# A new hand-fixed order of instructions and transfers in a two-branch state-space kernel

## The chip, the cores and the metric

One core of one Trainium2 chip. The metric is the device time of one execution in microseconds (us), taken over several runs; lower is better. Beside it stands one profiled execution, from which all rows of the trace come.

## The reference

Two independent branches, A and B, on 2048 time steps and 640 channels, are computed and put side by side in one output of 2048 x 1280 in bf16.

Branch A is a diagonal complex state-space layer: a projection of `x`, a linear recurrence over time for each of 640 states, and a projection back, of which the real part is kept.

```python
Lam_bar = jnp.exp(dt * Lam)
B_bar = ((Lam_bar - 1.0) / Lam)[:, None] * Bmat
Bu = jnp.einsum("bld,pd->blp", x + 0j, B_bar)
for t in range(L):
    h = Lam_bar[None, :] * h + Bu[:, t, :]
    hs.append(h)
y = 2.0 * jnp.einsum("blp,dp->bld", hseq, Cmat).real + x * Dskip[None, None, :]
```

Branch B filters `k` with four taps, multiplies by `v`, convolves each channel with a filter as long as the sequence (by Fourier transforms of twice the length), adds a skip and multiplies by `q`.

```python
k_shift = k_shift + k_pad[:, t:t + S, :] * shift_k[:, ks - 1 - t][None, None, :]
kv = k_shift * v
y_f = kv_f * kf_f[None, :, :, :]
y = irfft2(y_f)[:, 0, :S, :]
y = y + kv * ssm_D[None, None, :]
return q * y
```

## The kernel before

Branch A splits time into four phases (step modulo 4, `q` = 0 to 3) of 512 steps each, and states into five tiles of 128 (`j` = 0 to 4). `x1a`, `x1`, `x2`, `x3`, `x0` load `x` transposed, one phase each (L414). `bt*` transpose B on TensorE (L391) and `btf0`, `bte*` evict it. `z{q}{j}` projects a phase onto a state tile (L424, L436) and, except where VectorE does it (`zd2{j}`), folds in the phase before it with diagonal matrices (L439, L440); `ze{q}{j}` evicts it from PSUM on ScalarE (L795). For phase 0, `rs{j}` and `h0{j}` do the recurrence itself on VectorE with a scan between two rotations (L445 to L455), with tables that `tp{j}` (GpSimd) and `tab{j}` (ScalarE) make; `h{q}{j}` then gives the other phases (L484 to L488). `p{i}{q}` is the projection back (L499; L506 for the skip), for each of four time blocks `i`; `yo*` evict it and `yd*` store it. For some of them the skip is not in the matmul: `dbc` and `xn*` load what VectorE needs for it (`xd*`, L525). `CT*`, `ca*`, `cs*`, `gam` prepare C.

Branch B takes the channels in five groups of 128 (`G` = 0 to 4). Per group: `kT`, `vT` load `k` and `v` transposed (L551), `kS` copies `kT` across partitions (L558), `tap{G}_{m}` is the short filter (L584), `kv*` multiplies by `v` (L589, L595; `kve*` where ScalarE evicts first, L592), `kvo` writes the product to DRAM (L598) and `kvs` reads it back in another layout (L562); `hs` reads the long filter in that layout and `had` adds the skip to it. Then come two stages of a Fourier transform by matmuls for the filter and for the product, `s1h`, `s2h` and `s1k`, `s2k` (L607, L621 to L624), with evictions `s1he`, `s2he`, `s1ke`, `s2ke` on ScalarE (L611, L627). `y{G}_{half}` multiplies the two spectra on VectorE (L634 to L637), `inv{G}_{q}` is the inverse's first stage (L645 to L648), `zs` evicts it (L653), `zt` transposes it by a transfer (L658), `fin` is the second stage (L666), `qi` loads `q` (L661), `ob` multiplies by it (L671), `od_` stores (L687). The constants are made at the start: `gp*`, `G*`, `nG` for the transform, `H0` and `H1` (transposing transfers, L779) and `nH` for the inverse, `pp`, `aRM`, `dRM` for the small matrices.

Nothing is scheduled by a compiler. `make_plan` names 538 pieces, each with an engine, a cost in us, what it depends on, and, for matmuls, a PSUM slot that it takes until the piece that gives it back. `ORDER` is a text with all 538 names, found by a search over such costs; the kernel runs through it and calls each piece. `@n` behind a name is the slot: 0, 2, 4 and 6, each 1024 columns of f32. Every engine and every issuing queue executes its own pieces strictly in that order, and waits are put in from the data. All large transfers are issued by SP, in the order of the text.

Of the kernel before, what the change touches and what calls it, by code (L numbers as in the profile page):

```python
# [896 lines left out]


ORDER = """
pc wz l_ldt B0 wm0@0 l_lim l_lre B1 l_dsk dc zer gp2 wme0@0 x1a l_sk bt0@2 vt@0 x1 wm1@4 vc@0 pc2 bte0@2 exp btf0 gp3 rho wme1@4  # L900
bt1@0 bt2@4 B2 Fi bte1@0 skt@2 rr z10a@6 B3 G2 den B4 z10 bte2@4 Fq tp0 trig1 x2 skc@2 bt3@4 dD z11a@2 dS0 bte3@4 bt6@0 z11 tp1
bte6@0 ze10@6 kT0 bt5@4 lam ze11@2 bt4@0 z12@6 bte4@0 gp1 dL x3 G3 bt7@0 z21@2 gp0 bte5@4 tab0 dc2 z20@4 kS0 bte7@0 ze21@2 dcol
tp2 rden tab1 zd21 vT0 z22@2 ze20@4 gam ze12@6 CT0 tap0_1@4 G1 zd20 tap0_0@6 z14@0 ze22@2 tp3 tab2 kv0_0@6 z23@2 CT1 G0 kv0_1@4
tp4 ze14@0 z13@6 nG ze23@2 dS1 ca1 kT1 zd22 z30@2 pp ze13@6 ca0 x0 cs1 z31@6 tab4 cs0 aRM kS1 tab3 zd23 z24@0 hs0 ze31@6 ca2
kvo0 dRM z01@6 ca3 cs2 ze30@2 cs3 ze24@0 tap1_1@4 ze01@6 tap1_0@2 had0 zd24 s1h0_1@0 z00@6 kvs0 kve1_0@2 s1he0_1@0 vT1 dS2
kve1_1@4 rs1 ca4 s1h0_2@4 s1h0_3@0 z33@2 ze00@6 s1he0_3@0 s1he0_2@4 cs4 s1h0_0@0 s1k0_1@4 ze33@2 z34@6 hs1 kv1_0 s1ke0_1@4
s1he0_0@0 rs0 kT2 s1k0_3@0 s1k0_0@4 ze34@6 s2h0_2@2 kvo1 s1ke0_3@0 s2h0_3@6 s1ke0_0@4 z03@0 had1 s2he0_2@2 h01 s2he0_3@6 kS2 h00
s1h1_3@6 s1k0_2@2 ze03@0 s2h0_0@4 vT2 s1ke0_2@2 s2h0_1@0 rs3 s2he0_0@4 s2k0_2@2 kvs1 s2he0_1@0 s2k0_1@4 s2ke0_2@2 s2k0_0@0 H0
s1he1_3@6 s2k0_3@2 s2ke0_0@0 z32@6 h03 s2ke0_3@2 H1 s2ke0_1@4 y0_1 s1k1_3@4 qi0 s1h1_1@2 ze32@6 s1k1_0@0 s1ke1_3@4 tap2_1@6
s1he1_1@2 tap2_0@4 y0_0 z04@2 kve2_0@4 s1ke1_0@0 kve2_1@6 s1k1_2@0 s1k1_1@6 kv2_0 ze04@2 z02@4 s1ke1_2@0 nH kT3 rs4 s1ke1_1@6  # L910
s1h1_0@6 s1h1_2@0 ze02@4 dbc inv0_1@2 kvo2 s1he1_0@6 inv0_3@4 s1he1_2@0 inv0_0@6 rs2 kS3 zs0_3@4 s2k1_0@0 hs2 zs0_1@2 s2k1_1@4
s2ke1_0@0 kvs2 inv0_2@2 zs0_0@6 s2h1_1@0 zs0_2@2 s2h1_0@6 h04 xn2 s2he1_1@0 s2k1_3@2 s2ke1_1@4 zt0_0 s2k1_2@0 h02 s2ke1_3@2
s2h1_2@4 s2ke1_2@0 s2h1_3@2 h14 zt0_1 s2he1_2@4 p10@0 s2he1_0@6 s2he1_3@2 had2 y1_0 vT3 s1k2_2@2 s1k2_3@6 p00@4 s1ke2_2@2
s1ke2_3@6 xn1 yo10@0 dS3 y1_1 inv1_0@0 yo00@4 s1k2_0@6 yd00 s1k2_1@4 zs1_0@0 tap3_1@2 yd10 s1ke2_1@4 tap3_0@0 s1ke2_0@6 inv1_1@4
kv3_0@0 kT4 inv1_3@6 zs1_1@4 kv3_1@2 s2k2_1@0 zs1_3@6 h11 s1h2_0@4 kvo3 s1h2_2@2 p30@6 s1he2_0@4 s1he2_2@2 dS4 s2ke2_1@0 h10
s1h2_3@0 s1h2_1@2 yo30@6 fin0_1@4 hs3 s1he2_1@2 inv1_2@6 ob0_1@4 s1he2_3@0 s2k2_2@2 kS4 h12 zs1_2@6 s2k2_0@4 kvs3 s2ke2_2@2
s2k2_3@0 s2h2_1@6 h13 s2ke2_3@0 s2h2_0@2 zt1_1 s2ke2_0@4 s2h2_3@0 s2he2_0@2 had3 h31 s2h2_2@4 s2he2_1@6 vT4 p11@2 s2he2_2@4 y2_0
s2he2_3@0 s1k3_0@0 s1h3_1@4 yo11@2 fin0_0@6 s1ke3_0@0 p01@2 zt1_0 s1he3_1@4 ob0_0@6 y2_1 od_0 s1k3_3@6 s1k3_1@4 yo01@2 tap4_0@0
s1ke3_3@6 yd01 tap4_1@2 yd11 s1ke3_1@4 inv2_1@6 kv4_1@2 inv2_2@4 zs2_1@6 kv4_0@0 inv2_3@2 zs2_2@4 h32 s1h3_2@6 kvo4 s1h3_0@0 qi1
p20@4 s1he3_2@6 zs2_3@2 h23 s1he3_0@0 s1k3_2@0 s1h3_3@2 yo20@4 fin1_1@6 h30 hs4 s1ke3_2@0 inv2_0@4 s1he3_3@2 s2k3_1@0 kvs4  # L920
zs2_0@4 s2h3_1@2 ob1_1@6 s2ke3_1@0 s2k3_2@4 h33 zt2_1 s2he3_1@2 s2k3_0@6 s2ke3_2@4 fin1_0@0 s2h3_2@2 s2ke3_0@6 ob1_0@0 s2h3_3@4
s2he3_2@2 had4 s2k3_3@6 od_1 h34 s2he3_3@4 s2h3_0@2 s2ke3_3@6 s1k4_3@4 zt2_0 s1k4_1@0 s2he3_0@2 p21@6 y3_1 s1ke4_3@4 s1ke4_1@0
s1h4_2@0 s1k4_0@4 yo21@6 s1h4_3@2 y3_0 s1ke4_0@4 yd21 inv3_3@6 qi2 s1he4_3@2 inv3_2@4 s1he4_2@0 yd20 p03@2 xn3 zs3_3@6 h21
zs3_2@4 s1h4_0@4 s1k4_2@6 yo03@2 fin2_1@0 s1he4_0@4 inv3_0@2 ob2_1@0 s1ke4_2@6 inv3_1@4 h22 zs3_0@2 s2k4_2@6 zs3_1@4 s1h4_1@0
fin2_0@2 s1he4_1@0 zt3_1 s2k4_3@4 ob2_0@2 s2k4_1@0 s2ke4_3@4 h24 s2h4_2@2 od_2 s2ke4_2@6 s2h4_1@4 zt3_0 s2he4_2@2 s2h4_3@6 h20
s2ke4_1@0 s2h4_0@2 s2he4_3@6 s2k4_0@0 y4_1 p02@6 s2ke4_0@0 s2he4_1@4 qi3 s2he4_0@2 yd03 yd30 p31@4 yo02@6 y4_0 yd02 fin3_0@6
yo31@4 inv4_2@2 yd31 ob3_0@6 fin3_1@4 zs4_2@2 inv4_1@0 ob3_1@4 inv4_0@6 zs4_1@0 xd1 inv4_3@2 od_3 zs4_0@6 p22@0 zs4_3@2 xd2
zt4_1 p13@2 yo22@0 qi4 zt4_0 p12@0 yo13@2 yd13 fin4_1@2 yd22 yo12@0 p23@6 xd3 ob4_1@2 p33a@0 yo23@6 fin4_0@2 yd23 yo33a p32@6
yd12 ob4_0@2 yd33a od_4 p33 yo32@6 yd32 yo33@0 yd33
"""  # L930


# [66 lines left out]
```

## Time and profile before

| | us |
|---|---|
| median of 3 runs | 197.36 |
| lowest, highest run | 196.55, 197.95 |
| profiled execution, its own time | 198.36 |
| its span, first to last instruction | 196.6 |

The core was granted 0.998 of TensorE's clock over the span. Names of pieces are not in the trace; a piece is found by its line and by its place in the order. Times in the trace are us from the start of the span. In a row of a timeline the first number is the start, the second the length; a square bracket gives idle time before it and what ended it. SPq is the queue of SP as it issues transfers: the length of such a row is the time that issuing takes, not the transfer. In the rows on waits the numbers are the total, the count and the longest.

### The profile page before, as it was taken

What the parts mean: (1) busy time and instruction counts of PE and PEld (TensorE: products, weight loads), DVE (VectorE), ACT (ScalarE), POOL (GpSimd) and SP (SyncE); (2) the same over time, 40 slices, a digit from 0 to 9 for tenths busy, and PEclk for the clock granted to TensorE, in tenths of its full rate; (3) what the DMA queues carried; (4) which work ended last, traced back from release to release, by engine and by line L of the source; (5) the groups of instructions that cost most, each with busy time, mean ns of one, the idle gap of its engine ahead of it and who ended that gap; (6) DMA issues with size and microseconds to landing.
All of it is one profiled execution on the core that took longest, in us unless ns stands there. A gap on an engine that the chain in (4) does not pass through costs nothing.

```text
span 196.6 us, 5431 instructions
## 1 busy us (share of the span) xinstructions
PE 188.0 (96%) x2295; PEld 133.6 (68%) x2295; DVE 173.8 (88%) x289; ACT 150.9 (77%) x182; POOL 27.8 (14%) x54
## 2 busy tenths in 40 slices
...
GB/s 147 227 212 186 143 245 206 180 207 158 158 156 239 207 200 116 113 239 181 178 172 236 162 197 130 248 245 183 182 222 200 143 88 213 231 98 191 244 89 155
DMA packets 110810, 36.00 MB, mean 183 GB/s; under 512 B 104893, under 2 KB 109762, under 8 KB 110786
## 3 DMA queue, kind: packets, MB, share of 16 engines
q1 hardware_dynamic: 110736, 35.64, 90.7%
...
## 4 chain that ended last, share of the span: by engine, by line
PE 66%; SPq 11%; DMA 9%; ACT 8%; POOL 1%; issue 1%; DVE 1%; DVEq 0%; POOLq 0%
PE ps L499 20%; PE ps L436 9%; PE ps L607 5%; PE ps L621 4%; SPq L771 4%; PE ps L623 4%; PE ps L622 4%; PE ps L624 4%; DMA xT<-in_A_x_dram 3%; PE ps L584 3%; DMA vT<-in_B_v_dram 3%; PE ps L666 3%; DMA zz<-in_A_B_im_dram 2%; SPq L551 2%; PE ps L645 2%; ACT Hf L627 2%
## 5 line engine op out<-in xcount | busy, mean ns | idle before, releaser
L499 PE MATMUL ps<-Cs,F 128*128 128x320 bf16 x320 | 47.3, 299 | 0.0
L436 PE MATMUL ps<-xT,BT 128*128 128x512 bf16 x192 | 45.6, 379 | 1.6 <-DMA xT<-in_A_x_dram 1.6
L499 PEld LDWEIGHTS <-F 128*128 128x128 bf16 x320 | 29.8, 98 | 11.2 <-DVE F L448 0.5
L436 PEld LDWEIGHTS <-BT 128*128 128x128 bf16 x192 | 18.0, 98 | 23.5 <-issue 2.3
L795 ACT CAST F<-ps 128x1024 bf16<-128x1024 f32 x20 | 20.0, 1010 | 4.6 <-PE ps L440 3.3
L653 ACT CAST zz<-ps 128x1024 bf16<-128x1024 f32 x20 | 19.8, 1036 | 3.6 <-PE ps L648 2.3
L611 ACT CAST As_kv<-ps 128x1024 bf16<-128x1024 f32 x20 | 19.8, 1025 | 1.7 <-PE ps L607 1.2
L627 ACT CAST Xs<-ps 128x1024 bf16<-128x1024 f32 x20 | 20.1, 1062 | 1.3 <-PE ps L624 1.3
L611 ACT CAST As_h<-ps 128x1024 bf16<-128x1024 f32 x20 | 20.0, 1030 | 0.8 <-PE ps L607 0.8
L627 ACT CAST Hf<-ps 128x1024 bf16<-128x1024 f32 x20 | 19.9, 1064 | 0.0
L621 PE MATMUL ps<-As_kv,Gre 128*128 128x128 bf16 x80 | 17.5, 219 | 0.3 <-DVE vT L589 0.3
L646 PE MATMUL ps<-Xs,nHim 128*128 128x128 bf16 x80 | 17.5, 219 | 0.2 <-DVE Xs L637 0.2
L645 PE MATMUL ps<-Xs,Hre 128*128 128x128 bf16 x80 | 17.5, 219 | 0.0
L621 PE MATMUL ps<-As_h,Gre 128*128 128x128 bf16 x80 | 17.5, 219 | 0.0
L622 PE MATMUL ps<-As_h,nGim 128*128 128x128 bf16 x80 | 17.5, 219 | 0.0
L623 PE MATMUL ps<-As_h,Gim 128*128 128x128 bf16 x80 | 17.5, 219 | 0.0
L624 PE MATMUL ps<-As_h,Gre 128*128 128x128 bf16 x80 | 17.5, 219 | 0.0
L623 PE MATMUL ps<-As_kv,Gim 128*128 128x128 bf16 x80 | 17.5, 219 | 0.0
L624 PE MATMUL ps<-As_kv,Gre 128*128 128x128 bf16 x80 | 17.5, 219 | 0.0
L622 PE MATMUL ps<-As_kv,nGim 128*128 128x128 bf16 x80 | 17.5, 219 | 0.0
L648 PE MATMUL ps<-Xs,Hre 128*128 128x128 bf16 x80 | 17.5, 219 | 0.0
L647 PE MATMUL ps<-Xs,Him 128*128 128x128 bf16 x80 | 17.5, 219 | 0.0
...
## 6 DMA issues: line engine op xcount, KB each, us to landing
h_st<-in_B_ssm_k_dram SPq DMA_DIRECT2D x10, 256.0 KB, 4.1
kv_rows<-vT SPq DMA_DIRECT2D x5, 512.0 KB, 4.5
kv_st<-kv_rows SPq DMA_DIRECT2D x10, 256.0 KB, 5.3
qb<-in_B_q_dram SPq DMA_DIRECT2D x5, 512.0 KB, 5.7
out_dram<-qb SPq DMA_DIRECT2D x5, 512.0 KB, 4.2
...
```

The lines of the kernel that those rows point to most:

```text
L436: mm(ps[:, r, :], lhsT=self.BT[:, r, k, j * 128:(j + 1) * 128], rhs=xT[:, k, :], start=(k == 0), stop=(prev is None and k == NT - 1))
L499: mm(ps[:, b, 0:320], lhsT=self.F(p, j)[:, r, ts], rhs=self.Cs[:, r, j, c0:c0 + 320], start=(j == 0 and r == 0), stop=((i, p // 2) in SKD ...
L611: self.nc.scalar.copy(out=As[:].rearrange("p k (h s) -> p h k s", h=2)[:, :, :, 16 * q:16 * q + 16], in_=ps[:].rearrange("p h (k s) -> p h ...
L621: mm(o_re, lhsT=self.Gre[:, k1, :], rhs=re, start=True, stop=False)
L622: mm(o_re, lhsT=self.nGim[:, k1, :], rhs=im, start=False, stop=True)
L623: mm(o_im, lhsT=self.Gim[:, k1, :], rhs=re, start=True, stop=False)
L624: mm(o_im, lhsT=self.Gre[:, k1, :], rhs=im, start=False, stop=True)
L627: self.nc.scalar.copy(out=dst[:, :, o:o + 128 * n], in_=ps[:] if n == 4 else ps.rearrange("p (r n) -> p r n", r=2))
L645: mm(o_re, lhsT=self.Hre[:, k1, :], rhs=yre, start=True, stop=False)
L646: mm(o_re, lhsT=self.nHim[:, k1, :], rhs=yim, start=False, stop=True)
L653: self.nc.scalar.copy(out=self.Zs[:, :, 2 * ks[0]:2 * ks[0] + n, :].rearrange("p i k c -> p k i c"), in_=psf.rearrange("p (k i c) -> p k i ...
L795: A(f"ze{q}{j}", "ACT", EV, [f"z{q}{j}", "zer"], lambda ps, q=q, j=j: K.nc.scalar.copy(out=K.F(q, j), in_=ps[:]), give=f"z{q}{j}", group=f ...
```

## The change

Only the text of `ORDER` changes: the same 538 names in another sequence, and other slots for many of the matmuls. No function, cost, tile or dependency in the code is touched. The new text comes from a new run of the search, for which transfers and latencies were taken to be slightly longer than before. The first and the middle lines, before and after:

```diff
-pc wz l_ldt B0 wm0@0 l_lim l_lre B1 l_dsk dc zer gp2 wme0@0 x1a l_sk bt0@2 vt@0 x1 wm1@4 vc@0 pc2 bte0@2 exp btf0 gp3 rho wme1@4
-bt1@0 bt2@4 B2 Fi bte1@0 skt@2 rr z10a@6 B3 G2 den B4 z10 bte2@4 Fq tp0 trig1 x2 skc@2 bt3@4 dD z11a@2 dS0 bte3@4 bt6@0 z11 tp1
+wz B0 pc l_ldt wm0@0 l_lim l_lre B1 l_dsk pc2 dc zer gp0 wme0@0 x1a bt0@2 l_sk dc2 x1 vt@0 wm1@4 pp vc@0 bte0@2 exp rho bt2@0 Fi
+B2 rr skt@2 den btf0 wme1@4 bt1@6 aRM B3 gp3 z10a@4 skc@2 bte2@0 bte1@6 B4 G0 z10 x2 gp1 rden bt3@6 dS0 ze10@4 z11a@0 bte3@6 dRM
...
-s1he0_0@0 rs0 kT2 s1k0_3@0 s1k0_0@4 ze34@6 s2h0_2@2 kvo1 s1ke0_3@0 s2h0_3@6 s1ke0_0@4 z03@0 had1 s2he0_2@2 h01 s2he0_3@6 kS2 h00
-s1h1_3@6 s1k0_2@2 ze03@0 s2h0_0@4 vT2 s1ke0_2@2 s2h0_1@0 rs3 s2he0_0@4 s2k0_2@2 kvs1 s2he0_1@0 s2k0_1@4 s2ke0_2@2 s2k0_0@0 H0
+s1k0_1@2 z03@6 rs0 s1ke0_1@2 kT2 s1ke0_3@4 ze34@0 H1 s1k0_2@4 s1k0_0@0 ze03@6 s2h0_2@2 s1ke0_0@0 had1 s2h0_1@6 rs3 s1ke0_2@4 kS2
+s2h0_0@0 s2he0_2@2 kvo1 s2k0_1@4 s2he0_0@0 s2k0_0@2 s2he0_1@6 s2k0_3@0 s2ke0_1@4 nH s2k0_2@6 h00 s2ke0_0@2 s2h0_3@4 vT2
```

The order of SP alone, which the prediction uses most, from `x2` to `kT4`:

```text
before: x2 kT0 x3 kS0 dcol vT0 CT0 CT1 kT1 x0 kS1 hs0 kvo0 kvs0 vT1 hs1 kT2 kvo1 kS2 vT2 kvs1 H0 H1 qi0
        kT3 dbc kvo2 kS3 hs2 kvs2 xn2 zt0_0 zt0_1 vT3 xn1 yd00 yd10 kT4
after:  x2 kT0 dcol x3 kS0 vT0 CT0 CT1 kT1 x0 kS1 kvo0 hs0 H0 vT1 kvs0 hs1 kT2 H1 kS2 kvo1 vT2 kvs1 qi0
        kvo2 kT3 kvs2 kS3 hs2 vT3 zt0_1 xn2 zt0_0 xn3 kT4
```

From `kT4` on: before `kvo3 hs3 kS4 kvs3 zt1_1 vT4 zt1_0 od_0 yd01 yd11 kvo4 qi1 hs4 kvs4`, after `kvo3 yd10 kS4 kvs3 hs3 vT4 zt1_1 zt1_0 yd00 od_0 yd30 xn1 dbc qi1 kvo4 yd01 hs4 kvs4`.

The order of ScalarE at the start: before `exp btf0 bte1 rr G2 trig1 bte3 ze10 ze11 bte4 G3 bte5`, after `exp rr btf0 aRM bte1 G0 ze10 bte3 trig1 bte5 ze11 bte4`. The order of VectorE from `rs1`: before `rs1 cs4 kv1_0 rs0 had1 h01 h00 rs3 h03 y0_1 y0_0 kv2_0 nH rs4`, after `rs1 h01 cs4 kv1_0 rs0 had1 rs3 nH h00 h03 y0_0 y0_1 kv2_0 rs4`. On TensorE the pieces up to `z01` and up to `p10` are the same sets in both orders; between `z01` and `p10`:

```text
before: z01 tap1_1 tap1_0 s1h0_1 z00 s1h0_2 s1h0_3 z33 s1h0_0 s1k0_1 z34 s1k0_3 s1k0_0 s2h0_2 s2h0_3 z03 s1h1_3 s1k0_2
        s2h0_0 s2h0_1 s2k0_2 s2k0_1 s2k0_0 s2k0_3 z32 s1k1_3 s1h1_1 s1k1_0 tap2_1 tap2_0 z04 s1k1_2 s1k1_1 z02 s1h1_0
        s1h1_2 inv0_1 inv0_3 inv0_0 s2k1_0 s2k1_1 inv0_2 s2h1_1 s2h1_0 s2k1_3 s2k1_2 s2h1_2 s2h1_3 p10
after:  z01 tap1_0 tap1_1 z00 s1h0_3 s1h0_2 z33 s1h0_1 s1h0_0 z34 s1k0_3 s1k0_1 z03 s1k0_2 s1k0_0 s2h0_2 s2h0_1 s2h0_0
        s2k0_1 s2k0_0 s2k0_3 s2k0_2 s2h0_3 z32 s1h1_3 s1h1_1 tap2_0 tap2_1 z04 s1k1_1 s1h1_2 s1k1_3 s1k1_0 inv0_1 z02
        s1k1_2 s1h1_0 inv0_0 inv0_3 s2h1_3 s2h1_2 inv0_2 s2k1_1 s2k1_2 s2k1_0 s2h1_1 s2k1_3 s2h1_0 p10
```

More of the change, by code (lines that the diff above doesn't have):

```diff
@@ L899 @@
 ORDER = """
-pc wz l_ldt B0 wm0@0 l_lim l_lre B1 l_dsk dc zer gp2 wme0@0 x1a l_sk bt0@2 vt@0 x1 wm1@4 vc@0 pc2 bte0@2 exp btf0 gp3 rho wme1@4
-bt1@0 bt2@4 B2 Fi bte1@0 skt@2 rr z10a@6 B3 G2 den B4 z10 bte2@4 Fq tp0 trig1 x2 skc@2 bt3@4 dD z11a@2 dS0 bte3@4 bt6@0 z11 tp1
-bte6@0 ze10@6 kT0 bt5@4 lam ze11@2 bt4@0 z12@6 bte4@0 gp1 dL x3 G3 bt7@0 z21@2 gp0 bte5@4 tab0 dc2 z20@4 kS0 bte7@0 ze21@2 dcol
-tp2 rden tab1 zd21 vT0 z22@2 ze20@4 gam ze12@6 CT0 tap0_1@4 G1 zd20 tap0_0@6 z14@0 ze22@2 tp3 tab2 kv0_0@6 z23@2 CT1 G0 kv0_1@4
@@ L904 @@
-tp4 ze14@0 z13@6 nG ze23@2 dS1 ca1 kT1 zd22 z30@2 pp ze13@6 ca0 x0 cs1 z31@6 tab4 cs0 aRM kS1 tab3 zd23 z24@0 hs0 ze31@6 ca2
-kvo0 dRM z01@6 ca3 cs2 ze30@2 cs3 ze24@0 tap1_1@4 ze01@6 tap1_0@2 had0 zd24 s1h0_1@0 z00@6 kvs0 kve1_0@2 s1he0_1@0 vT1 dS2
-kve1_1@4 rs1 ca4 s1h0_2@4 s1h0_3@0 z33@2 ze00@6 s1he0_3@0 s1he0_2@4 cs4 s1h0_0@0 s1k0_1@4 ze33@2 z34@6 hs1 kv1_0 s1ke0_1@4
-s1he0_0@0 rs0 kT2 s1k0_3@0 s1k0_0@4 ze34@6 s2h0_2@2 kvo1 s1ke0_3@0 s2h0_3@6 s1ke0_0@4 z03@0 had1 s2he0_2@2 h01 s2he0_3@6 kS2 h00
@@ L908 @@
-s1h1_3@6 s1k0_2@2 ze03@0 s2h0_0@4 vT2 s1ke0_2@2 s2h0_1@0 rs3 s2he0_0@4 s2k0_2@2 kvs1 s2he0_1@0 s2k0_1@4 s2ke0_2@2 s2k0_0@0 H0
-s1he1_3@6 s2k0_3@2 s2ke0_0@0 z32@6 h03 s2ke0_3@2 H1 s2ke0_1@4 y0_1 s1k1_3@4 qi0 s1h1_1@2 ze32@6 s1k1_0@0 s1ke1_3@4 tap2_1@6
-s1he1_1@2 tap2_0@4 y0_0 z04@2 kve2_0@4 s1ke1_0@0 kve2_1@6 s1k1_2@0 s1k1_1@6 kv2_0 ze04@2 z02@4 s1ke1_2@0 nH kT3 rs4 s1ke1_1@6
-s1h1_0@6 s1h1_2@0 ze02@4 dbc inv0_1@2 kvo2 s1he1_0@6 inv0_3@4 s1he1_2@0 inv0_0@6 rs2 kS3 zs0_3@4 s2k1_0@0 hs2 zs0_1@2 s2k1_1@4
@@ L912 @@
[L912 to L927, printed above, removed]
@@ L928 @@
-zt4_1 p13@2 yo22@0 qi4 zt4_0 p12@0 yo13@2 yd13 fin4_1@2 yd22 yo12@0 p23@6 xd3 ob4_1@2 p33a@0 yo23@6 fin4_0@2 yd23 yo33a p32@6
-yd12 ob4_0@2 yd33a od_4 p33 yo32@6 yd32 yo33@0 yd33
+wz B0 pc l_ldt wm0@0 l_lim l_lre B1 l_dsk pc2 dc zer gp0 wme0@0 x1a bt0@2 l_sk dc2 x1 vt@0 wm1@4 pp vc@0 bte0@2 exp rho bt2@0 Fi
+B2 rr skt@2 den btf0 wme1@4 bt1@6 aRM B3 gp3 z10a@4 skc@2 bte2@0 bte1@6 B4 G0 z10 x2 gp1 rden bt3@6 dS0 ze10@4 z11a@0 bte3@6 dRM
+bt6@2 z11 Fq tp1 bte6@2 trig1 kT0 bt5@6 dD bt7@4 z12@2 bte7@4 bte5@6 tp0 dcol lam ze11@0 x3 bt4@6 z21@4 dL bte4@6 gp2 ze12@2
@@ new lines @@
+z22@6 ze21@4 kS0 tab1 zd21 vT0 z24@4 tp3 ze22@6 tab0 CT0 zd22 z20@6 G2 gam tap0_1@2 ze20@6 tap0_0@0 ze24@4 kv0_1@2 CT1 z14@6 G1
+zd20 tp2 G3 z31@2 kv0_0@0 kT1 ze14@6 dS1 ca0 z13@6 zd24 x0 ca1 z30@0 cs0 tab2 ze13@6 tp4 kS1 cs1 ze31@2 kvo0 z23@6 ca2 hs0 tab3
+cs2 z01@2 ze23@6 H0 nG ca3 zd23 ze30@0 tap1_0@6 vT1 ze01@2 tap1_1@4 cs3 tab4 z00@0 kve1_1@4 dS2 kvs0 had0 kve1_0@6 rs1 s1h0_3@6
+s1h0_2@4 ze00@0 z33@2 s1he0_3@6 s1he0_2@4 ca4 h01 s1h0_1@4 s1h0_0@6 z34@0 s1he0_0@6 hs1 cs4 s1he0_1@4 ze33@2 kv1_0 s1k0_3@4
@@ new lines @@
+s1k0_1@2 z03@6 rs0 s1ke0_1@2 kT2 s1ke0_3@4 ze34@0 H1 s1k0_2@4 s1k0_0@0 ze03@6 s2h0_2@2 s1ke0_0@0 had1 s2h0_1@6 rs3 s1ke0_2@4 kS2
+s2h0_0@0 s2he0_2@2 kvo1 s2k0_1@4 s2he0_0@0 s2k0_0@2 s2he0_1@6 s2k0_3@0 s2ke0_1@4 nH s2k0_2@6 h00 s2ke0_0@2 s2h0_3@4 vT2
+s2ke0_3@0 z32@2 s2ke0_2@6 h03 s2he0_3@4 kvs1 y0_0 s1h1_3@4 qi0 s1h1_1@6 ze32@2 tap2_0@0 s1he1_3@4 tap2_1@2 z04@4 kve2_1@2 y0_1
+kve2_0@0 s1he1_1@6 s1k1_1@0 s1h1_2@6 ze04@4 s1k1_3@2 s1ke1_3@2 s1k1_0@4 kv2_0 s1ke1_1@0 inv0_1@2 rs4 kvo2 z02@0 zs0_1@2 kT3
@@ new lines @@
+s1he1_2@6 s1ke1_0@4 s1k1_2@6 s1h1_0@4 ze02@0 inv0_0@2 kvs2 h04 s1he1_0@4 inv0_3@0 zs0_0@2 s2h1_3@4 zs0_3@0 rs2 s2h1_2@2 kS3
+s1ke1_2@6 inv0_2@0 hs2 s2he1_3@4 s2k1_1@6 s2he1_2@2 vT3 s2k1_2@4 s2ke1_1@6 s2k1_0@2 h02 s2ke1_2@4 s2h1_1@6 zs0_2@0 s2k1_3@4
+s2he1_1@6 dS3 zt0_1 s2h1_0@0 h14 s2ke1_0@2 p10@6 s2he1_0@0 xn2 s2ke1_3@4 y1_0 zt0_0 s1k2_1@4 s1k2_0@0 p00@2 s1ke2_0@0 xn3
+s1ke2_1@4 y1_1 yo10@6 s1k2_3@6 s1k2_2@4 yo00@2 tap3_1@0 s1ke2_3@6 tap3_0@2 s1ke2_2@4 inv1_0@6 kT4 had2 kv3_0@2 inv1_1@4 zs1_0@6
```

15 lines of the change are left out of this document (added).

## The prediction

> **What bounds the kernel now.** I read the busy time first, then the transfer queue, then the chain that ended last, then the waits.
>
> ```profile
> PE 188.0 (96%) x2295; PEld 133.6 (68%) x2295; DVE 173.8 (88%) x289; ACT 150.9 (77%) x182; POOL 27.8 (14%) x54
> ...
> q1 hardware_dynamic: 110736, 35.64, 90.7%
> ```
>
> Four resources are nearly full at once: TensorE at 96%, the transfers at 90.7% of 16 engines' span, VectorE at 88%, ScalarE at 77%. A busy TensorE is not yet a full one, so I work out from the chain how long its matmuls take at their dense pitch:
>
> ```profile
> 13.39 0.86 PE ps L391 x12
> ...
> 40.89 1.25 PE ps L436 x5
> ...
> 42.58 1.08 PE ps L436 x5
> ...
> 44.09 1.85 PE ps L584 x32
> ...
> 49.41 0.55 PE ps L607 x16
> ...
> 57.33 0.16 PE ps L621
> ...
> 59.22 1.08 PE ps L436 x5
> ...
> 89.56 2.75 ACT Xs L627 x3
> ...
> 109.05 1.36 PE ps L499 x10
> ...
> 111.10 0.57 PE ps L666 x16
> ...
> 192.69 0.49 DVE yo L534
> ```
>
> A matmul with 512 columns costs 1.08/5 = 0.216 us; 192 of L436, 40 of L439 and L440 and 8 of L424 make 51.8. L499: 320 x 0.136 = 43.5. The twelve groups of L621 to L624 and L645 to L648 hold 960 matmuls; 32 of them lie between 57.33 and 59.22, 0.059 each, so 56.7. L607: 320 x 0.55/16 = 11.0. L584: 160 x 1.85/32 = 9.3. L666: 160 x 0.57/16 = 5.7. The 135 that are left (transposes, warm-up, diagonal products) go by L391, 0.072 each: 9.7. Together about 187.7 us.
>
> ```profile
> 1.19 2.31 PE L151 MATMUL ps<-diagL 128*128 128x512 bf16 x5 [1.19 <-DVE kT L217]
> ...
> 17.14 6.63 PE L436 MATMUL ps<-xT,BT 128*128 128x512 bf16 x30 [0.64 <-DMA xT<-in_A_x_dram]
> ```
>
> TensorE begins at 1.19 and is done when VectorE's last eviction starts, at 192.69, so it has 191.5 us for 187.7 us of matmuls. That is the frame of everything below: the instructions do not change, so no order can gain more than about 3.8 us (2%) unless the start or the tail also shrinks, while a loss has no such bound. The waits that TensorE and its feeders do have are these:
>
> ```profile
> PE ps L436 <- DMA xT<-in_A_x_dram: 1.6, 3, 0.6
> ...
> DVE vT L589 <- DMA vT<-in_B_v_dram: 2.1, 2, 1.6
> ...
> ACT zz L653 <- DMA zz<-zz: 1.3, 1, 1.3
> ...
> PE ps L584 <- ACT zz L653: 0.4, 1, 0.4
> ...
> PE ps L584 <- ACT F L795: 0.3, 1, 0.3
> ```
>
> By the Trainium skill (Perfetto Trace Analysis, Identifying the Most-Contended Engine) matmul busy time is a poor measure and the weight loads' share a better one: that is 68% here, below VectorE's 88%, and the time would follow VectorE, which, followed below in the same way, reaches the last filter product (y4_1) 0.6 us earlier: -0.6 instead of +0.4. The pitches above speak against it: they are taken from issue to issue, and still fill 187.7 of 191.5 us.
>
> **The change part by part.** Every edit is a move, so a part costs only what it makes somebody wait. I compare the two orders at places where the same instructions have gone before on TensorE; there only waits can differ.
>
> *Start, 0 to 40.89 us.* On SP all transfers up to x0 stay ahead of it; only dcol moves ahead of x3 and kS0. The sum of the issues is unchanged, so x0 still arrives for 40.89, where TensorE already waited. On ScalarE the evictions of B's transposes (btf0, bte1) now stand behind rr, and bte1 also behind the table load and aRM, and G0 comes ahead of ze10:
>
> ```profile
> 5.58 1.07 ACT L397 CAST BT<-ps 128x512 bf16<-128x512 f32 x2 [0.45 <-DVE BT L399]
> 6.76 0.22 ACT L285 ACTIVATE rr<-rho 128x20 f32<-128x20 f32 x1
> 6.98 1.28 ACT L375 ACT_TABLE_LOAD   x1
> ...
> 10.09 0.20 ACT L288 ACTIVATE sin<-Fq 128x15 f32<-128x15 int32 x1
> ...
> 10.72 1.01 ACT L397 CAST BT<-ps 128x1024 bf16<-128x1024 f32 x1
> ```
>
> rr is ready at 6.76 as before. Then btf0 (about 0.6, half of 1.07 and its latency), the load (1.28), aRM (four small activations; trig1's three took 10.72 - 10.09 = 0.63, so about 0.9), bte1 (0.6): bte1 ends near 10.2 instead of 6.65. z10 reaches the piece that needs it near 9.2, so TensorE waits about 1.1 us. The cover is the two later waits for x: 0.64 at 17.14, and the rest of the 1.6 us (0.5) at 40.89. That is 1.1 against 1.1, so I book 0; without that cover it would be +1.1. The eight evictions after it (bte3, ze11, bte4, bte5, ze12, ze21, ze22, ze20) I followed one by one: each frees its PSUM slot before TensorE comes to it, the tightest being ze13 ahead of z23, with about 0.8 us.
>
> *40.89 us to p10.* The sets before p10 are the same in both orders. Before has p10 at 92.4. ScalarE evicts one 1024-column tile every 2.75/3 = 0.92 us, TensorE makes one in 16 x 0.056 to 0.059, so the two run side by side and the order of slots matters. Followed tile by tile, TensorE in the new order is 0.5 us ahead at z32 (it no longer stands on s1h0_1 and on L795's 0.3), and then gives most of it back: s1k1_0 waits about 0.35 for ze04 and inv0_1 about 0.6 for s1ke1_3. At p10 it is 0.1 ahead. VectorE gets there the same: h02 is due at 92.2.
>
> *The SP queue in the same stretch* is what I trust least. H0 and H1 come forward, H0 between hs0 and vT1, H1 between kT2 and kS2, and kvo1 now stands directly ahead of vT2, which waits for it to land:
>
> ```profile
> 41.70 0.60 SPq L598 DMA_DIRECT2D kv_rows<-vT  x1
> 46.65 1.31 SPq L562 DMA_DIRECT2D kv_st<-kv_rows  x2
> 48.00 3.53 SPq L551 DMA_TRANSPOSE vT<-in_B_v_dram  x1
> ...
> 55.71 2.81 SPq L551 DMA_TRANSPOSE kT<-in_B_k_dram  x1
> ...
> 60.50 1.28 SPq L558 DMA_DIRECT2D kS<-kT  x2
> 61.88 1.87 SPq L551 DMA_TRANSPOSE vT<-in_B_v_dram  x1
> 63.85 1.34 SPq L562 DMA_DIRECT2D kv_st<-kv_rows  x2
> 65.24 4.70 SPq L779 DMA_TRANSPOSE Hre<-Gre  x1
> 69.99 2.20 SPq L779 DMA_TRANSPOSE Him<-nGim  x1
> ...
> kv_rows<-vT SPq DMA_DIRECT2D x5, 512.0 KB, 4.5
> kv_st<-kv_rows SPq DMA_DIRECT2D x10, 256.0 KB, 5.3
> ```
>
> H0 (2.2 to 4.7) lies mostly in the hole from 42.3 to 46.65, where the queue waited for kvo0 to land. vT1 then passes kvs0: kvs0 is issued at 46.4 to 50.4 and lands by 51.7 to 55.7; s1k0_3 wants it at 55.9. That is just covered. kvs1 is worse. kT2 waits for kv1_0 on VectorE, which has h01 in front of it now:
>
> ```profile
> 54.41 1.22 DVE L595 TENSOR_TENSOR vT<-kT,vT 128x2048 bf16<-128x2048 bf16 x1
> ...
> 59.91 0.69 DVE L445 TENSOR_TENSOR rot<-tabs,F 128x1024 bf16<-128x1024 bf16 x1
> ...
> 62.03 0.69 DVE L445 TENSOR_TENSOR rot<-tabs,F 128x1024 bf16<-128x1024 bf16 x1
> ```
>
> h01 is 62.03 - 59.91 = 2.1 us, but VectorE has less left in front of it (zd24 is done earlier, nG only moved), so kv1_0 comes about 0.8 later. kT2 at 56.5, +2.8; H1 +2.2 to 4.7; kS2 +1.3; kvo1 issued at 62.8 to 65.3, landed 4.5 later at 67.3 to 69.8; vT2 +1.9 to 3.5; kvs1 issued at 69.2 to 73.3, its second half landed about 0.7 + 5.3 later: 75.2 to 79.3. TensorE asks for it (s1k1_1) at 75.7, with inv0_1 and z02 queued behind. Below zero is excluded, since an early kvs1 is not used earlier. I take H1 near its lower row, 2.2, because like that row it follows one transpose of its size and not a gather: 0.8 us, from a bound of 0 to 3.6.
>
> By the Trainium skill (DMA: Bandwidth & Descriptors, Issuing engines are not separate DMA queues) starting a transfer takes little beside the transfer itself; then moving H1 would not hold kvs1 back, and the sum would be -0.4. The rows above disagree: one transpose of 512 KB held SP for 4.70 us, the next for 2.20.
>
> *p10 to the end.* vT3 moves ahead of zt0 (issued near 90 instead of 98.9), which removes what is left of VectorE's 2.1 us on vT (0.5) and, with both zt0 still due by 101, most of ScalarE's 1.3 on zz. Next late there is kv3_0 itself, on which inv1_3 now waits for its PSUM slot, so only 0.3 us reach TensorE. qi1 falls behind yd00, yd30, xn1 and dbc and may hold ob1_1 for up to 1.8 us; VectorE is about 0.9 ahead there, and I book 0. h30 goes ahead of y3_0, which delays it by one step, and inv3_0 is one step later as well. The tail (inv4, then the same five full projections and p33 in two halves, the two zt4 swapped) keeps its sum: 0.
>
> Sum: 0 (start) - 0.1 (p10) + 0.8 (kvs1) - 0.3 (after) = +0.4 us on a span of 196.6. The profiled execution's own time, 198.36, is 1.0 above the median of the runs, 197.36, so I carry the difference over to the median: 197.8.
>
> **The rivals.** *The new order starves TensorE in the middle (slower).* If H1 costs what Hre cost, 4.7, and vT2 3.5, kvs1 lands at 79.3 and TensorE stands for 3.6 us at s1k1_1. Nothing makes it up, because the 187.7 us behind are dense: +0.4 + 2.8 = +3.2, so 200.6. It decides from a landing of 77.3 on. For it: 90.7% of the transfer time is used and H1 is added ahead of kvs1. Against: before left holes in that queue (42.3 to 46.65) which H0 fills. Chance 0.33, with the smaller waits of this sort (kvs0, qi1) among it.
>
> *The waits on transfers vanish (faster).* If transfers arrive as the rows' lower ends say, kvs1 costs nothing (-0.8), the 1.3 on zz and the 0.5 on vT reach TensorE in full (-1.5 more than booked) and the 0.4 of L584 on zz goes: +0.4 - 2.7 = -2.3, so 195.1. Against: ScalarE and VectorE stand next in line at these places. Chance 0.22.
>
> *The queue holds nothing up.* kvs1 costs 0 and all else is as booked: -0.4, 197.0. Chance 0.11; it is the sum that the rule on issuing gives.
>
> **How the numbers follow.** The forecast, +0.4, has 0.34. A change within 1% (2 us, about what a measurement of this kernel tells from none) holds the forecast and the queue case, 0.45; slower by over 1% is 0.33, the starved case, and faster 0.22. With both signs that likely, the likeliest case has a range of its own: 197.0 (kvs1 at its early end) to 199.5 (kvs1 near the point from which the starved case decides, with the 1.1 us of the start half uncovered). The whole range goes down to 195.0, the faster case, and up to 201.5, the starved case with 0.9 for a late qi1, half of its 1.8.
>
> **What would show it.** Right: L436 of z01 starts at 40.9 again with some wait for xT left; z10 shows about 1 us of waiting for BT L397; L607 on kv_st has a wait for the transfer kv_rows near 76; p10 (L499) begins between 92 and 94. Wrong: z01 starting later than 41.5 (the cover of the start was not there), a wait on Hre or nHim at L645 or on qb at L671 of more than 2 us, VectorE idle for over 2 us between 45 and 165, or a tail from inv4 to the last store that differs from before's.

## The result and the profile after

| | before | after |
|---|---|---|
| median of 22 runs each, us | 197.76 | 198.59 |
| lowest, highest run, us | 195.73, 201.01 | 197.38, 199.87 |
| profiled execution, its own time, us | 198.36 | 197.9 |
| its span, us | 196.6 | 196.0 |

The ratio of the times is 1.005 (95% interval 1.0028 to 1.0071): the new order is slower by about 1.0 us, 0.5%, with 0.6 to 1.4 us in the interval; the medians differ by 0.83 us. A ratio is not the quotient of the two medians shown beside it, and it leaves out single executions that ran over 1.5% above the fastest of their kernel. The two profiled executions stand the other way round, 0.6 us of span in favour of the new order. That is no contradiction, since a profile is one execution out of a spread of several us; it means that span against span tells nothing here. What can be compared between profiles are stretches: from one place to a later one, ahead of each of which TensorE has done the same work in both orders.

The page of the profile after has the same four nearly full resources.

```profile
PE 188.2 (96%) x2295; PEld 133.3 (68%) x2295; DVE 175.3 (89%) x289; ACT 150.8 (77%) x182; POOL 26.0 (13%) x54
...
q1 hardware_dynamic: 110736, 35.64, 92.2%
```

TensorE's timeline of the changed kernel, at the places that the prediction names: z10's wait, z21, z01 with its first diagonal product (L439), p10.

```profile
9.77 1.04 PE L436 MATMUL ps<-xT,BT 128*128 128x512 bf16 x4 [0.42 <-ACT BT L397]
...
17.01 1.25 PE L436 MATMUL ps<-xT,BT 128*128 128x512 bf16 x5 [0.21 <-DMA xT<-in_A_x_dram]
...
40.59 1.25 PE L436 MATMUL ps<-xT,BT 128*128 128x512 bf16 x5 [0.30 <-DMA xT<-in_A_x_dram]
41.68 0.38 PE L439 MATMUL ps<-F,diagL 128*128 128x512 bf16 x1
...
92.64 1.52 PE L499 MATMUL ps<-Cs,F 128*128 128x320 bf16 x10
```

The same two last places in the kernel before:

```profile
41.98 0.38 PE L439 MATMUL ps<-F,diagL 128*128 128x512 bf16 x1
...
92.40 1.79 PE L499 MATMUL ps<-Cs,F 128*128 128x320 bf16 x10
```

Three things are to be seen. z10 waits for BT, which it did not before, and the waits for x behind it are still there, only shorter. z01 is 0.30 us earlier than before (40.59 against 40.89). From z01's first L439 to p10 the new order needs 92.64 - 41.68 = 50.96 us and the old one 92.40 - 41.98 = 50.42: the middle, forecast 0.1 us shorter without the transfer kvs1, is 0.54 us longer.

The waits of the changed kernel, in totals, counts and longest, give the rest: one on a load of h_st (L568), which the prediction did not speak of.

```profile
PE ps L436 <- DMA xT<-in_A_x_dram: 1.0, 3, 0.5
...
DVE h_st L568 <- DMA h_st<-in_B_ssm_k_dram: 0.6, 1, 0.6
...
PE ps L436 <- ACT BT L397: 0.4, 1, 0.4
...
PE ps L621 <- DVE qb L671: 0.2, 1, 0.2
```

No row has L607 waiting for the transfer kv_rows, the +0.8 of the sum. SP's queue in the stretch shows why.

```profile
41.58 4.07 SPq L779 DMA_TRANSPOSE Hre<-Gre  x1
...
56.15 2.33 SPq L551 DMA_TRANSPOSE kT<-in_B_k_dram  x1
58.53 2.42 SPq L779 DMA_TRANSPOSE Him<-nGim  x1
...
62.38 0.60 SPq L598 DMA_DIRECT2D kv_rows<-vT  x1
65.58 1.93 SPq L551 DMA_TRANSPOSE vT<-in_B_v_dram  x1
67.61 1.32 SPq L562 DMA_DIRECT2D kv_st<-kv_rows  x2
```

H1 costs 2.42, close to the 2.2 that was taken for it. But vT2, which waits for kvo1 to land, is issued at 65.58, 3.2 us behind kvo1, not 4.5, and kvs1 goes out at 67.61, 1.6 us ahead of the early end of the forecast (69.2).

### The profile page after: what moved, and what is told of

Same layout as the page of the kernel before. It is cut to its first block, busy times and chain, and to the rows that moved or that the text cites. A ratio compares the mean times of both kernels' runs of the same rounds, so it can differ in the third digit from the quotient of the medians.

```text
span 196.0 us, 5429 instructions
## 1 busy us (share of the span) xinstructions
PE 188.2 (96%) x2295; PEld 133.3 (68%) x2295; DVE 175.3 (89%) x289; ACT 150.8 (77%) x182; POOL 26.0 (13%) x54
## 4 chain that ended last, share of the span: by engine, by line
PE 68%; SPq 15%; DMA 8%; DVE 5%; issue 1%; ACT 1%; DVEq 0%
PE ps L499 21%; PE ps L436 9%; SPq L414 6%; PE ps L607 5%; PE ps L621 4%; PE ps L584 4%; SPq L771 4%; PE ps L623 4%; PE ps L622 4%; PE ps L624 4%; SPq L551 3%; DMA xT<-in_A_x_dram 3%; DMA h_st<-in_B_ssm_k_dram 3%; PE ps L666 2%; PE ps L645 2%; PE ps L646 2%
## 5 line engine op out<-in xcount | busy, mean ns | idle before, releaser
L499 PE MATMUL ps<-Cs,F 128*128 128x320 bf16 x320 | 47.0, 299 | 0.0
L499 PEld LDWEIGHTS <-F 128*128 128x128 bf16 x320 | 29.9, 98 | 10.7
L795 ACT CAST F<-ps 128x1024 bf16<-128x1024 f32 x20 | 20.0, 1011 | 3.7 <-PE ps L440 2.5
L627 ACT CAST Hf<-ps 128x1024 bf16<-128x1024 f32 x20 | 20.4, 1075 | 0.7 <-PE ps L624 0.7
```

Of the source, the lines that this page charges most:

```text
L499: mm(ps[:, b, 0:320], lhsT=self.F(p, j)[:, r, ts], rhs=self.Cs[:, r, j, c0:c0 + 320], start=(j == 0 and r == 0), stop=((i, p // 2) in SKD ...
L627: self.nc.scalar.copy(out=dst[:, :, o:o + 128 * n], in_=ps[:] if n == 4 else ps.rearrange("p (r n) -> p r n", r=2))
L795: A(f"ze{q}{j}", "ACT", EV, [f"z{q}{j}", "zer"], lambda ps, q=q, j=j: K.nc.scalar.copy(out=K.F(q, j), in_=ps[:]), give=f"z{q}{j}", group=f ...
```

## The experiments

All runs are timed in five rounds against the kernel before, on the same chip. "Old" is the order before, "new" the order after. Where two orders are joined, the names that are left follow in the second order's sequence, and PSUM slots are renumbered behind the joint.

Three theories were put down ahead of the first runs: A, a transfer (kvs1 above all) lands late in some executions; B, the second half of the new order gives back what the first half gains; C, the difference is one of chip and day. After them came two more: S, the loss is at the start, where z10's wait for bte1, booked at 0 because later waits for x cover it, is not covered in most executions; R, it lies behind z01, in the order of matmuls and evictions or in a transfer that comes late there.

**Both orders, and each half.** Four kernels: the changed kernel again, the new order up to p30 with the old behind, the reverse, and, on another chip, the kernel before as its own control.

```diff
 the new order up to p30, then the old (at the joint)
-zs1_3@2 s2k2_1@4 yd10 p30@2 s2ke2_1@4 h12 kS4 s1he2_0@0 s1he2_2@6
+dbc xn1 yd00 p30@2 s1he2_0@0 s1he2_2@6 dS4 s2ke2_1@4 h10
 the old order up to p30, then the new
-kvo3 s1h2_2@2 p30@6 s1he2_0@4 s1he2_2@2 dS4 s2ke2_1@0 h10
+kvo3 s1h2_2@2 xn3 p30@6 s2ke2_1@0 h12 kS4 s1he2_0@4 s1he2_2@2
```

> The changed kernel as it is, on another chip and with a profile of its own. Measured so far: 1.005 of before, about +0.8 us, while its one profile ends TensorE at 192.64 us, as before's does (192.65). Theory A (a transfer lands late in some executions, kvs1 ahead of s1k1_1 above all): ratio 1.003 to 1.007, and this second profile shows a wait of 0.5 us or more on kv_rows or another transfer at s1k1_1 in some place where the first shows none. Theory B (the loss lies in the second half, where the gain of the first half is given back): same ratio, p30 again about 0.9 us earlier than in before's profile and the first inverse of group 4 (inv4) level with it or later. Theory C (the difference is of chip and day, not of the order): ratio 0.998 to 1.002.

> The new order up to p30 (the first projection of time block 3, about 106 us), and from there the order of before, with the PSUM slots renamed so that they fit at the seam. Theory A (late transfers between 40 and 76 us): the whole loss comes along, ratio 1.003 to 1.007. Theory B (the first half gains, the second half loses): the 0.9 us by which the new order is ahead at p30 stays, ratio 0.993 to 0.998, and it beats both kernels. Theory C: 0.998 to 1.002 with p30 early but the gain lost at y4, whose VectorE work sets inv4.

> The order of before up to p30, and the new order from there. Theory A: nothing of the loss is left, ratio 0.998 to 1.002. Theory B: the loss of the second half stands alone, about +0.9 + 0.8 us, ratio 1.005 to 1.010. Theory C: 0.998 to 1.002.

> The kernel of before, unchanged, as a control, and for a second profile of it. All three kernels so far measured about 1.006, though their profiles end within 0.2 us of before's or ahead of it, and the order in both halves by itself cost as much as in both together. If that is a difference of the orders, this one gives 0.998 to 1.002. If a kernel that is timed beside before is always found slower by this much, it gives 1.004 to 1.008. In its profile: the stretch from z01 to p33 within 0.8 us of the first profile's 150.1 us, and z01 between 39 and 41 us.

| kernel | ratio | 95% interval | median, us | before beside it, us |
|---|---|---|---|---|
| the changed kernel again | 1.0062 | 1.0037 to 1.0086 | 197.3 | 196.28 |
| new up to p30, then old | 1.0058 | 1.0036 to 1.0079 | 197.47 | 196.28 |
| old up to p30, then new | 1.0062 | 1.0039 to 1.0085 | 197.42 | 196.28 |
| the kernel before again | 1.0000 | 0.9969 to 1.0031 | 197.46 | 197.33 |

The loss is there a second time and the control has none. But each half alone seems to lose as much as both together, so halves do not add up, and ratios alone will not place the loss. None of the three theories is the whole of it: C falls with the second loss and the control, A asked for no loss with the old first half, and B for a gain with the new one. One part of the third kernel's loss is of the joint's making. Behind it TensorE has a wait for ob0 that no profile of its two parents shows:

```profile
112.47 0.63 PE L666 MATMUL ps<-Mq,zz 128*128 128x64 bf16 x16 [0.49 <-DVE qb L671]
```

The timelines ahead of the joint do better. TensorE in the second profile of the changed kernel (z10, z21, z01, p10):

```profile
9.83 1.04 PE L436 MATMUL ps<-xT,BT 128*128 128x512 bf16 x4 [0.74 <-ACT BT L397]
...
16.69 8.80 PE L436 MATMUL ps<-xT,BT 128*128 128x512 bf16 x39
...
40.89 0.38 PE L439 MATMUL ps<-F,diagL 128*128 128x512 bf16 x1
...
91.84 1.52 PE L499 MATMUL ps<-Cs,F 128*128 128x320 bf16 x10
```

And in the kernel with the old order up to p30 (z21, z01, p10):

```profile
16.14 6.64 PE L436 MATMUL ps<-xT,BT 128*128 128x512 bf16 x30
...
40.34 0.38 PE L439 MATMUL ps<-F,diagL 128*128 128x512 bf16 x1
...
90.75 1.52 PE L499 MATMUL ps<-Cs,F 128*128 128x320 bf16 x10
```

In these two executions neither z21 nor z01 waits for x: the brackets of before and after are gone. So they show what the orders do without that cover. z21 begins at 16.69 in the new order and at 16.14 in the old, 0.55 us apart. Up to 0.20 of that may be x1, which z10 has at 8.71 in the first and at 8.51 in the second; the rest is z10's wait. From z21 to L439 both need 24.20 us, and from L439 to p10 the new order 50.95, the old 50.41. The 0.54 us of the middle have come a second time, to the hundredth. Both executions are the fastest of their kernel (196.28 of 10 runs with a median of 197.3, 196.36 of 12 with 197.42), so they need not show all that the others lose.

**The start alone.** New up to z01 and then old, and the reverse.

```diff
 the new order up to z01, then the old
-cs2 z01@2 ze23@6 H0 nG ca3 zd23 ze30@0 tap1_0@6
+zd23 z01@6 ca3 ze30@0 cs3 tap1_1@4 ze01@6 tap1_0@2 had0
 the old order up to z01, then the new
-z01@6 ca3 cs2 ze30@2 cs3 ze24@0 tap1_1@4
+cs2 z01@4 H0 ca3 ze30@2 tap1_0@6 vT1 ze01@4 tap1_1@2
```

> The new order up to z01 (the first matmul that needs x0, about 40 us), the order of before from there. Theory S (the loss is at the start: dcol ahead of x3, ScalarE's and GpSimd's new order, and x0 lands later): ratio 1.003 to 1.008. Theory R (the loss lies in the rest, in transfers that land late in some executions): 0.998 to 1.002.

> The order of before up to z01, the new order from there. Theory S: 0.998 to 1.002. Theory R: 1.003 to 1.008, and its profile shows waits of together 0.5 us or more between z01 and p33 that the best profile of the new order (149.85 us from z01 to p33) does not have.

The new start gave 1.0082 (1.005 to 1.0114; 199.07 against 197.33 us), the old start 1.0032 (1.0005 to 1.0059; 198.09). S asked for the first to be slower and the second level, R for the reverse; both are slower. The first carries a wait that neither parent has, at the joint, for had0:

```profile
47.96 0.40 PE L607 MATMUL ps<-R,h_st 64*128 64x128 bf16 x8 [1.22 <-DVE h_st L568]
```

1.2 of 197.3 us is 0.6%, most of its 0.8%, so it says little of the start. The second has no such wait at its joint, and no wait for BT at z10, and is still slower. Its VectorE and then its TensorE show another place:

```profile
141.00 0.23 DVE L568 TENSOR_TENSOR h_st<-h_st,dcol_b 128x16 bf16<-128x16 bf16 x1 [1.21 <-DMA h_st<-in_B_ssm_k_dram]
```

```profile
142.39 0.22 PE L621 MATMUL ps<-As_kv,Gre 128*128 128x128 bf16 x1 [0.80 <-DVE qb L671]
```

had4 waits 1.21 us for its load hs4, ob1_0 is queued behind it on VectorE, and s2k3_1 on TensorE needs the PSUM slot that ob1_0 gives back. In the first profile of the changed kernel this was 0.59 us on VectorE, in the second it did not occur.

**Taking out the two waits.** aRM moved behind bte1 on ScalarE; had4 moved behind h21 on VectorE; both.

```diff
 aRM behind bte1
-wme1@4 bt1@6 aRM B3 gp3 z10a@4 skc@2 bte2@0 bte1@6 B4
+wme1@4 bt1@6 B3 gp3 z10a@4 skc@2 bte2@0 bte1@6 aRM B4
 had4 behind h21
-had4 ob1_0@0 s2he3_0@6 s2k3_0@2 s2he3_3@4 h21 od_1
+ob1_0@0 s2he3_0@6 s2k3_0@2 s2he3_3@4 h21 had4 od_1
```

> The new order with one move: on ScalarE the eviction bte1 goes ahead of aRM again (and so of the table load), so that z10 need not wait for it. Theory S' (the 0.4 to 0.8 us for which z10 waits on BT L397 are paid whenever x2 and x0 come early enough, so that TensorE and not x0 sets the start of z01): no wait on BT L397 in the profile, ratio 0.3 to 0.4% below the new order's, 1.001 to 1.003. Theory R (the loss lies behind z01): the wait is gone too, and the ratio stays at 1.004 to 1.007.

> The new order with one move: on VectorE the small addition had4, which waits for the transfer hs4, goes behind ob1_0 and h21, so that ob1_0 frees its PSUM slot for s2k3_1 without waiting for hs4. The three profiles with the new second half that hold this place show waits of 0, 0.6 and 1.2 us there. Theory R: that wait is gone, TensorE goes on at s2k3_1 without the 0.4 to 0.8 us on qb L671, ratio 1.002 to 1.004. Theory S': the wait is gone, and the ratio stays at 1.004 to 1.007.

> Both moves together. If S' and R each hold a part, 0.998 to 1.001, level with before or ahead of it; if neither is the cause, 1.004 to 1.007 again.

The first gave 1.0077 (1.005 to 1.0103; 197.91 against 196.09 us), the second 1.0044 (1.0018 to 1.007), both 1.005 (1.0024 to 1.0076). By what was put down for both together, 1.005 is the answer that neither move is the cause. Moving had4 takes away 0.0027 beside the other move, with intervals that overlap. Moving aRM does not help, but its profile does not show why, since that execution was late ahead of the place of the move. These are rows of TensorE, first of the changed kernel, then with aRM moved, and the eviction on ScalarE that follows in the latter:

```profile
4.42 0.97 PE L151 MATMUL ps<-diagL 128*128 128x512 bf16 x3
...
5.77 0.64 PE L189 MATMUL ps<-ident,zz 5*64 5x5 bf16 x16
```

```profile
4.78 1.46 PE L151 MATMUL ps<-diagL 128*128 128x512 bf16 x3
...
6.98 0.64 PE L189 MATMUL ps<-ident,zz 5*64 5x5 bf16 x16
```

```profile
7.67 1.07 ACT L397 CAST BT<-ps 128x512 bf16<-128x512 f32 x2 [1.21 <-PE ps L189]
```

```profile
14.60 0.72 PE L391 MATMUL ps<-ident,zz 128*128 128x128 bf16 x10 [1.57 <-ACT BT L397]
```

z10 waits no longer. But btf0 now begins at 7.67, right behind the small transposes of L189 (skt), which TensorE reached 1.21 us later than in the changed kernel although the move leaves its order alone: it was 0.36 us late at L151 already, whose three matmuls then took 1.46 us in place of 0.97. From btf0 on everything on ScalarE is late by this (ze10 at 12.65 against 11.43), and so the transposes of bt5 find slot 6 still taken by bt3, for 1.57 us. The kernel with both moves shows the same (1.11 us ahead of btf0, 1.15 at bt5). So these two profiles do not tell what the move is worth.

The rows show something else that the prediction and these moves passed over: in all seven profiles that have the new start's btf0 behind skt, btf0 begins 0.04 to 0.05 us after L189 ends, and its row names L189. btf0 reads what bt0 left in slot 2, and skt, which takes the same slot, stands ahead of it in the new order. This costs ScalarE 0.24 to 0.36 us in four of these profiles and 0.70 to 1.21 in three, ahead of bte1.

**The evictions where the kernel before has them.** bt1's transposes go right behind wm1, and btf0 and bte1 right behind exp, in the time in which ScalarE waits for rho (so btf0 is ahead of skt again); the same with had4 moved; and the old start with had4 moved.

```diff
-vt@0 wm1@4 pp vc@0 bte0@2 exp rho bt2@0 Fi B2 rr skt@2 den btf0 wme1@4 bt1@6 aRM B3 gp3 z10a@4 skc@2 bte2@0 bte1@6 B4
+vt@0 wm1@4 bt1@6 pp vc@0 bte0@2 exp btf0 bte1@6 rho bt2@0 Fi B2 rr skt@2 den wme1@4 aRM B3 gp3 z10a@4 skc@2 bte2@0 B4
```

> The changed kernel, but with the evictions at its start back where the kernel before has them: bt1's transposes right behind wm1 on TensorE, btf0 and bte1 right behind exp on ScalarE, in the time in which rr waits for rho. If the loss is at the start (z10 waits for bte1, 0.4 to 0.8 us in the profiles of the new order): no wait for BT L397 at z10, TensorE's lag from z10 to bt3 down from 1.2 to 1.7 us to about 0.5, and a ratio of 1.000 to 1.003. If the loss lies behind z01, or is spread over the order: 1.004 to 1.007, as the four forms of the new order so far.

> The same, with had4 behind h21 as well. If start and had4's wait for its load are the whole loss: 0.998 to 1.001, and in the profile neither a wait for BT L397 at z10 nor one of VectorE for hs4. If had4 is worth nothing: equal to the run with the old evictions alone, within 0.002.

> The order of the kernel before up to z01, the new one from there, and had4 behind h21. The same cut without the move of had4 gave 1.0032 with VectorE waiting 1.2 us for hs4. If had4 is what the new order loses behind z01: 0.998 to 1.001, no wait for hs4, and about 150.0 us from z01 to p33 in place of 151.4. If something else behind z01 is slower: 1.002 to 1.004 again.

They gave 1.0006 (0.9975 to 1.0038), 1.0012 (0.998 to 1.0043) and 1.0008 (0.998 to 1.0037), with medians of 197.93, 197.45 and 197.7 us beside 197.63. By the ratios none is faster than the kernel before; by the medians the second is 0.18 us faster. had4 reads as worth nothing between the first two, and as 0.0024 between the third and the same cut without its move (1.0032, on another chip), with intervals that overlap. In the third's profile the wait for hs4 is gone, and from z01's L439 to the end of the last L499 it takes 150.92 us, in place of 151.75 without the move. By the ratios the first is what the theory of the start asked for, and yet two things keep me from taking it as shown. The changed kernel itself did not run on this chip, and the intervals reach into the one that it had elsewhere (from 1.0028). And the second kernel's TensorE (z10, z21, z01, p10) shows where a gain at the start goes:

```profile
8.78 1.46 PE L436 MATMUL ps<-xT,BT 128*128 128x512 bf16 x6 [0.46 <-DMA xT<-in_A_x_dram]
...
16.61 8.81 PE L436 MATMUL ps<-xT,BT 128*128 128x512 bf16 x40 [0.26 <-DMA xT<-in_A_x_dram]
...
40.81 0.38 PE L439 MATMUL ps<-F,diagL 128*128 128x512 bf16 x1
...
91.76 1.52 PE L499 MATMUL ps<-Cs,F 128*128 128x320 bf16 x10
```

The wait for BT is gone, all six matmuls of z10 run in one piece, and then z21 waits 0.26 us for x2 and starts at 16.61: 0.08 us earlier than the changed kernel in its second profile, which did have the wait. The middle needs 91.76 - 40.81 = 50.95 again. So in this execution the edit gained next to nothing, and the parity of the three ratios is not explained by the profiles. The third kernel's profile says the same: old start, new middle, and from its L439 at 41.18 to p10 at 92.14 it takes 50.96.

## Why the prediction came out as it did

A change within 1% was forecast, in a range of 197.0 to 199.5, and 198.59 was measured; the +0.4 itself lies below the measured interval of 0.6 to 1.4 us. That the sum came this near is in part luck: two of its four terms were wrong, in opposite directions, the middle by 0.64 us and kvs1 by 0.8.

**The middle without kvs1, forecast -0.1, is +0.54.** This is the step that failed, and the best settled one. All ten profiles with the new middle need 50.95 or 50.96 us from L439 to p10, three of the four with the old middle (the kernel before twice, old up to p30) 50.41 or 50.42; the fourth, the new start, has its 1.22 us for had0 there. No row of the others has TensorE waiting for a transfer in this stretch. TensorE's busy time in one stretch of it, in us behind the length of the stretch, before and then after:

```profile
68.00:83.00 15.00, 14.68 (x159) 7.92 (x157) 14.48 (x20) 12.94 (x14) 0.00 (x0) 1.00 0.78 140
```

```profile
68.00:83.00 15.00, 14.16 (x157) 7.42 (x156) 14.51 (x19) 13.15 (x15) 0.00 (x0) 1.00 0.80 145
```

0.52 us less, at the same granted clock. From 40.89 to 68 TensorE is busy without a gap in both. The two waits of the new order in the stretch are these (s1k1_0, then inv0_1; s1k1_1 is the row before them):

```profile
76.13 0.40 PE L607 MATMUL ps<-R,kv_st 64*128 64x128 bf16 x8
...
77.30 0.40 PE L607 MATMUL ps<-R,kv_st 64*128 64x128 bf16 x8 [0.33 <-ACT F L795]
78.21 0.22 PE L645 MATMUL ps<-Xs,Hre 128*128 128x128 bf16 x1 [0.51 <-ACT As_kv L611]
```

They were forecast as 0.35 and 0.6, at the right places with the right releasers, and stand in all ten profiles as 0.32 to 0.33 and 0.51 to 0.52. (In the two kernels with the old start the second names VectorE's Xs, L637, at the same 0.52, so a faster s1ke1_3 alone need not remove it there.) The old order's one wait in the stretch:

```profile
72.39 0.37 PE L584 MATMUL ps<-kT,diagS 64*64 64x512 bf16 x1 [0.32 <-ACT F L795]
```

Wrong in the forecast was what stood against these waits, "0.5 us ahead at z32". z32 is a place where the sets are not the same: the old order has s1h1_3 ahead of it, the new one behind. Eight matmuls of L607 take 0.55/2 = 0.28 us by the prediction's own row, so over half of the lead was work not yet done. (In the profiles the lead at z32 is 67.47 - 41.68 against 68.10 - 41.98, 0.33 us, of which 0.28 is that work; on s1h0_1 TensorE stands in neither order.) The 0.3 on L795, counted into the lead at z32, lies behind z32 in the kernel before, at tap2_1: it is the 0.32 us above. What is left of 0.33 + 0.51 is 0.84 - 0.32 = +0.52.

**kvs1, forecast +0.8, is 0.** L607 at 76.13 has no wait. The term was built from H1's issue, which was right, and from kvo1's landing, for which the median over five transfers of 4.5 was taken; here it took at most 3.2 (3.5 to 3.9 in four more profiles of orders with this stretch, where TensorE has no wait for kvs1 either). With this alone kvs1 comes 1.3 us earlier, and its wait is gone. The starved middle, the rival at 0.33, falls with it; H0's 4.07 us lie at 41.58 to 45.65, mostly in the hole from 42.3 on. The rival at 0.11, by which the queue holds nothing up, had kvs1 right, and the time wrong for the middle's sake.

**The start, forecast 0, is 0 to +0.55, by when x lands.** bte1 ended at 9.71 (forecast 10.2, where the terms given there add up to 10.4), and z10 waited 0.42 to 0.82 us (forecast 1.1). The prediction had rr at 6.76 as before; it ran at 5.96, since in the kernel before it had stood behind the evictions. ScalarE of the changed kernel, btf0, the table load and bte1:

```profile
6.45 0.59 ACT L397 CAST BT<-ps 128x512 bf16<-128x512 f32 x1 [0.28 <-PE ps L189]
...
7.19 1.28 ACT L164 ACT_TABLE_LOAD   x1
...
9.15 0.56 ACT L397 CAST BT<-ps 128x512 bf16<-128x512 f32 x1
```

The cover is real, but a matter of each execution. Where x2 lands after 16.7, z21 waits for it in either order and the start costs nothing: in the first pair of profiles the new order is even 0.13 us earlier at z21 (17.01 against 17.14). Where x2 is early, up to 0.55 us stay, as the pair shows in which z21 and z01 do not wait for x. The prediction gave the price without cover as 1.1, which is twice that. How often it is paid in the 22 runs, the profiles cannot tell.

**Behind p10, forecast -0.3, is -1.6 to +0.5.** From p10 to the end of TensorE's last L499 the kernel before takes 100.26 and, in its second profile, 100.85 us; the changed kernel 100.00 and 99.26; the old start with the new order behind z01, in the profile with 1.21 us on hs4, 100.79. The gain on vT and zz is there (2.1 us of VectorE's waits on the loads of vT and 1.3 of ScalarE's on zz have no row in the changed kernel's two profiles), and had4, which stands ahead of ob1_0 in the new order and behind it in the old one, takes it back when hs4 lands late. This wait was not in the prediction at all.

Together, by the profiles: 0 to 0.55 (start), +0.54 (middle), 0 (kvs1) and -1.6 to +0.5 (behind p10), where the second and the third term are settled and the others vary from one execution to the next. Their span, -1.1 to +1.6, holds the measured +1.0, but does not single it out. What stays open: how the start and hs4 share what is left above 0.54, and why the old order up to p30 with the new one behind it was slower by 0.6%, though it has the old start, the old middle and no wait for hs4 in its profile: the 0.49 us of its joint are 0.25%.

That the 0.54 us reach the end of the kernel is argued, not shown. The old middle in the new order, which would test them in a time and not only in timelines, was not tried. Two pairs of runs differ in the stretch from z01 to p30 and little else: new up to z01 (1.0082) and new up to p30 (1.0058), old up to p30 (1.0062) and old up to z01 (1.0032). In both pairs the kernel with the new middle has the lower ratio, but on another chip, with intervals that overlap, and the other one carries a joint's wait, 1.22 and 0.49 us. Less these, if they count in full in every execution, the new middle is 0.4% slower in the first pair and level in the second. The times do not decide it.

Of the two rules of the Trainium skill, the one that takes the weight loads' share for the measure (Perfetto Trace Analysis, Identifying the Most-Contended Engine) gave -0.6, which the prediction states without its working and which has the wrong sign; the Trainium skill names that share beside MFU, which was not worked out here. The weight loads are at 68% again, and the 0.54 us were lost on TensorE at places where it stood idle. The one by which starting a transfer takes little (DMA: Bandwidth & Descriptors, Issuing engines are not separate DMA queues) gave a sum without kvs1, and kvs1 was indeed on time. But the rows still speak against it: H0 and H1 held SP for 4.07 and 2.42 us.
